# Float64 weight conversion in half pieces, six pieces cast on GpSimd, and x loads queued behind a slice's weights

## The chip, the cores and the metric

The kernel runs on one core of one Trainium2 chip. The metric is the device time of one execution in microseconds (us); with several runs the median is given. A core has TensorE (matrix products; "PE" in the profile, its weight loads "PEld"), VectorE ("DVE"), ScalarE ("ACT"), GpSimd ("POOL") and SyncE ("SP"), whose queue issues nearly all DMA transfers. Each engine works through its own instructions in their order. TensorE's granted clock has two levels, 1.2 and 2.4 GHz; the profile gives its mean in a stretch as a share of the higher one.

## The reference

Three parts in a row: attention with a decay, a gated FFN whose weights are float64, and a mixture of eight experts whose gate is balanced over tokens and experts.

```python
scores = scale * np.matmul(q, k.transpose(0, 1, 3, 2))
scores = np.where(causal, -1000000000.0, scores + decay)
attn = np.exp(scores - max) / sum              # 4 batches, 8 heads, 576 x 64
x = np.matmul(attn, v)                          # to 2304 tokens x 512
g, val = x @ w_gate, x @ w_val                  # 512 -> 1536, weights in float64
x = (silu(g) * val) @ w_out
logits = x @ moe2_w_gate                        # 8 experts
P = softmax, then 8 rounds of dividing by sums over experts and over tokens
out = sum over e of P[:, e] * (max(x @ w1[e], 0) @ w2[e])    # 512 -> 1024 -> 512
```

Every product is made from three fp32r products: each operand is a high word (a cast to fp32r) and a low word, the rest of the subtraction (`rest`).

## The kernel before

Attention of batch 0 runs alone (to about 75 us). Then attention of batch n+1 and the first FFN of batch n run merged, step by step, by a list of costs (`merge`): the first such pair to 247 us, the other two to 540 us, and the FFN of the last batch to 675 us. From there the second FFN runs in three phases over the tokens (to 1188, about 1660 and 2143 us), each phase through all slices of the experts' weights, forwards or backwards. Phase 0 reads the experts' weights (`w1`, `w2`), builds their word and sum forms and saves them to DRAM (`save` into `wq`); phases 1 and 2 read those forms back, slice by slice (`back`: `w1h`, `w1l`, `w2h`, `w2l`, `sh`, `sl`).

**Conversion.** The first FFN's weights lie in DRAM as the bits of float64, in 18 pieces of 128 partitions x 1024 values (4096 16-bit words). [...] The steps of a piece:

- the load `st<-wf` (L114, on SP; tile `st` in three buffers, and `st4` for every fourth piece, so that the load of a piece waits for an earlier piece's last reader);
- VectorE masks the exponent of the top word into `lead` (L129);
- ScalarE scales and rebases it with a Relu (L131);
- VectorE puts the sign back in `lead` (L132, 16-bit, 1024 columns) and shifts the middle word and joins it with `lead` (L134, 32-bit, 1024 columns), after which `v`, a view of `st`, holds fp32 values;
- for each half of 512 columns ScalarE casts to the high word (L139) and GpSimd subtracts for the low word (L167, `rest`), both into a tile of the ring `w` (6 buffers);
- the finished piece is stored to DRAM as `wsplit`, 1 MB, for the other three batches: pieces 0 to 5 in one go after batch 0's attention (L648), the later ones at once (L144).

Pieces 0 to 5 are converted at fixed points of batch 0's attention (`TURNS`; `ROWS` has six entries, so `i < len(ROWS)` means pieces 0 to 5) and kept in `w` as `ready` for the first FFN products; pieces 6 to 17 are converted by `load(s)` inside `moe_unit(0)`, one slice ahead of its use. A scheduler places the instructions of an engine by its own model of times, within the dependences and the orders that `issue_after` sets, so an instruction of piece 8 can stand inside batch 0's attention.

**Attention's names.** `ps_s` scores, `np`/`mn` (L297 on VectorE: decay, mask and row maximum; L302 on ScalarE: exponentials and their sums), `ps_t`/`pt` (transposes of the exponentials and their copies to SBUF, L423, L431, L436), `ps_o` (product with v, L451), `bt` (output, L455, L465), `xh`/`xl` (its high and low word, the FFN's input). In the FFN `pm` are the up products, `th`, `ah`, `al` the activation and its words, `py` the down products (L175 is the line of all three-term products).

**Translation of x.** The second FFN multiplies 2x2 blocks in seven products instead of eight, and its input is kept in DRAM (`xd`) and brought into seven forms by `xlate(2)` for phase 2 (`xload` and `xforms` make those of phases 0 and 1). It has four parts: two loads `xq<-xd` (L750), four subtractions on VectorE (L699), then seven times a cast to `h` on ScalarE (L734), a `rest` on GpSimd and a store `xo<-h` (L738). `h` has two buffers, so the third cast of a part waits for the first store to land. `last_w[0]` is the last weight load of phase 0 that `load2` issued; `issue_after(last_w[0].ins)` keeps an instruction behind it in the queue. In the second FFN `pa` are the up products (L937), which ScalarE moves to SBUF as `u` (L944).

Of the kernel before, what the change touches and what calls it, by code (L numbers as in the profile page):

```python
# [8 lines left out]
F32 = mybir.dt.float32  # L9
# [5 lines left out]
ALU = mybir.AluOpType  # L15
# [18 lines left out]
def attention_two_ffns(ctx: ExitStack, tc: tile.TileContext, qkT, vt, f, wf, g2, w1, w2, out):  # L34
    nc = tc.nc
# [11 lines left out]
    HP = 512  # L47
# [31 lines left out]
    for rows, c in ((slice(0, 64), 0), (slice(64, P), 64)):  # L79
        nc.vector.tensor_copy(out=maskd[rows], in_=maskf[rows, rows])  # L80
        nc.vector.tensor_reduce(
            out=picks[rows], in_=ident[rows, c:c + 3 * NG].rearrange("p (n j) -> p n j", j=3),
# [24 lines left out]
    def wload0(i, behind=None):  # L107
        if i % 4 == 2:
            st = stp.tile([P, 8 * HP + 4], U16, tag="st4", name="st4")
        else:  # L110
            st = cvp.tile([P, 8 * HP + 4], U16, tag="st", name="st", bufs=3)
        behind = behind or last_st[0]
        with tc.issue_after(behind.ins):
            last_st[0] = nc.sync.dma_start(out=st[:, 1:1 + 8 * HP], in_=wf[i].bitcast(U16))  # L114
        return st

    def convert(i):
        base = bases[:, 1:2] if i % 3 == 2 else bases[:, 0:1]
        W = 2 * HP
        st = sts.pop(i, None) or wload0(i)  # L120

        def words(dt):
            return st.bitcast(dt)[:, 0:2 * W].rearrange("p (i t) -> p i t", t=2)[:, :, 1]
        mid, v = words(U32), words(F32)
        top = st[:, 4:4 + 4 * W].rearrange("p (i t) -> p i t", t=4)[:, :, 0]
        lead = leads[i % 2]
        g = lead.bitcast(U16).rearrange("p (i t) -> p i t", t=2)[:, :, 1]
        with tc.issue_after(rows[i].ins) if i < len(ROWS) else ExitStack():
            nc.vector.tensor_scalar(out=g, in0=top, scalar1=0x7fff, scalar2=None, op0=ALU.bitwise_and)  # L129

        nc.scalar.activation(out=g, in_=g, func=AF.Relu, scale=8.0, bias=base)  # L131
        nc.vector.scalar_tensor_tensor(  # L132
            out=g, in0=top, scalar=0x8000, in1=g, op0=ALU.bitwise_and, op1=ALU.bitwise_or)
        nc.vector.scalar_tensor_tensor(  # L134
            out=mid, in0=mid, scalar=13, in1=lead, op0=ALU.logical_shift_right, op1=ALU.bitwise_or)
        t = wring.tile([P, 2, 2, HP], F32R, tag="w", name="w")
        halves = [slice(j * HP, (j + 1) * HP) for j in range(2)]
        for j, h in enumerate(halves):
            nc.scalar.copy(out=t[:, j, 0], in_=v[:, h])  # L139
            rest(t[:, j, 1], v[:, h], t[:, j, 0])  # L140
        if i < len(ROWS):
            stores.append((i, t))
        else:
            nc.sync.dma_start(out=wsplit[i], in_=t.bitcast(F32))  # L144
        return t
# [9 lines left out]
    ROWS = (3, 8, 15, 18, 22, 25)  # L155
# [9 lines left out]
    def rest(out, src, hi, eng=None):  # L165

        return (eng or nc.gpsimd).tensor_tensor(out=out, in0=src, in1=hi.bitcast(F32), op=ALU.subtract)  # L167
# [43 lines left out]
    for j in range(3):  # L211
        src = left if j else ct[0:B * H]
# [4 lines left out]
    for e in range(2):  # L217
        spread_in = nc.sync.dma_start(
            out=spread[64 * e:64 * e + 3 * NG],
            in_=cumt[16 * e:16 * e + NG].rearrange("n j s -> (n j) s"))  # L220
# [402 lines left out]
    with ExitStack() as hold:  # L623
        room = banks(hold, 2, 3)
        idle = room[1].tile([P, 512], F32, tag="t", name="idle")
        for _ in range(WARM):
            nc.tensor.matmul(out=idle[:, 0:P], lhsT=ident, rhs=ident, start=True, stop=True)
        for n, (_, fn) in enumerate(attn_unit(0, *room)):
            fn()
            for i in LOADS.get(n, ()):  # L630
                sts[i] = wload0(i, spread_in if i == 1 else last_qk[0])
            if n in ROWS:
                rows.append(last_step[0])
            if n in TURNS:
                w0.append(convert(len(w0)))
# [10 lines left out]
    with tc.issue_after(last_qk[0].ins):  # L646
        for i, t in stores:
            nc.sync.dma_start(out=wsplit[i], in_=t.bitcast(F32))  # L648
    merge(second, moe_unit(0, convert, w0), lead=LA)
    first.close()  # L650
    cdp = at_ctx.enter_context(pool("cdp", 2, side="right"))
# [43 lines left out]
    def xsums(quarters, ts):  # L695
        b11, b12, b21, b22 = quarters
        t4, t1, t2, t3 = ts
        for o, x, y in ((t1, b12, b11), (t3, b22, b12), (t2, b22, t1), (t4, b21, t2)):
            nc.vector.tensor_tensor(out=o, in0=x, in1=y, op=ALU.subtract)  # L699
        return b11, b21, b22, t4, t1, t2, t3  # L700
# [28 lines left out]
    def xwords(srcs, n, place):  # L729
        hs_ = []  # L730
        for f in range(NF + 1):
            if f < NF:
                hs_.append(sk.tile([P, 2, HG], F32R, tag="h", name="h", bufs=2)[:, :, 0:n])
                nc.scalar.copy(out=hs_[f][:, 0], in_=srcs[f])  # L734
            if f:
                h = hs_[f - 1]
                rest_next(h[:, 1], srcs[f - 1], h[:, 0])
                nc.sync.dma_start(out=place(f - 1), in_=h.bitcast(F32))  # L738
                yield

    def xlate(p):

        n = HG // 2
        for k in range(2):
            for c in range(2):
                st = wst.tile([P, KD, FS], F32, tag="w1", name="xq")[:, :, 0:n].rearrange("p (i j) n -> p i j n", i=2)
                for j in range(2):
                    b, n0 = divmod(p * GT + j * HG + c * n, S)
                    src = xd[b].rearrange("p (i k) n -> p i k n", i=2)[:, :, k, n0:n0 + n]
                    nc.sync.dma_start(out=st[:, :, j], in_=src)  # L750
                yield
                t = wst.tile([P, FS // P, DM], F32, tag="w2", name="xu").rearrange("p f (c n) -> p (f c) n", c=2)
                quarters = [st[:, i, j] for i in range(2) for j in range(2)]
                srcs = xsums(quarters, [t[:, i, 0:n] for i in range(4)])
                yield
                cols = slice(c * n, (c + 1) * n)
                yield from xwords(srcs, n, lambda f: xo[p][:, f, :, k, cols])
# [29 lines left out]
    last_w = [None]  # L787
# [26 lines left out]
    def keep1(i, ts):  # L814
        w1s[slices[i][1:]] = [t.rearrange("p k (f c) -> p f k c", f=NF) for t in ts]
        return w1s[slices[i][1:]]
# [75 lines left out]
    def back(n, i):  # L892
        if i >= len(slices) or i % NS < 2 or i < NS:
            return
        key = slices[i][1:]
        ts = (tiles1, tiles2)[n](i)
        for t, src in zip(ts, wq[(n,) + key]):
            nc.sync.dma_start(out=t.bitcast(F32), in_=src)
        if n:
            w2s[key] = ts  # L900
        else:
            keep1(i, ts)

    def weights(i):
        if i == NS:
            save(1, i - 1)
        back(0, i + 1)
        back(1, i - 1)
# [283 lines left out]
    def ending():  # L1192
        i = len(slices) - 1
        back(1, i)
        for f in zipped(fast(i - 1), form(i)):
            f()
        for t in range(TP):
            slow(i, t)
# [55 lines left out]
    list(make(0, 0))  # L1254
    later = xforms(1)
    last = xlate(2)
    for i in range(len(slices)):
        if i == NS:
# [13 lines left out]
        if 24 <= i < 24 + TP:  # L1272
            t = i - 24
# [42 lines left out]
```

## Time and profile before

| | |
|---|---|
| median of 3 runs | 2146.72 us (2146.15 to 2149.76) |
| the profiled execution | 2145.42 us, of it 2143.6 us span |
| TensorE busy | 2117.2 us, 99%, mean granted clock 0.997 |
| VectorE busy | 1387.9 us, 65% |
| ScalarE busy | 966.5 us, 45% |
| GpSimd busy | 1314.9 us, 61% |
| DMA | 558.09 MB, mean 260 GB/s |

The times come from whole executions; the span is from the first to the last instruction in the trace. Busy shares are means over stages with different limits. In the rows below a time is in us; "DVE lead L129 <- DMA st<-wf" reads: VectorE's instruction of line 129, which writes `lead`, stood idle until a DMA that wrote `st` had landed. Lines are those of the kernel before. In the changed kernel L132 and L134 are L136 and L138, L139 is L140, L167 is L170, and lines behind are 3 or 4 higher.

### The profile page before, as it was taken

The numbers are of one execution on the slowest core, as the hardware profiler recorded it, in microseconds if no ns is written. First come the engines' busy times: TensorE is split into PE (matmuls) and PEld (weight loads), VectorE is DVE, ScalarE is ACT, GpSimd is POOL, SyncE is SP. The second block draws the span as 40 slices with busy tenths as digits, with TensorE's granted clock in tenths as the row PEclk, the third lists the DMA queues.
The fourth block names the chain that finished last, engine by engine and source line by source line (L and its number), as shares of the span: only waits on it lengthen the run. The fifth ranks groups of instructions, "written<-read, shape, count | busy, mean of one in ns | idle before, by whom it ended". The sixth has DMA issues, their size and how long they took to land.

```text
span 2143.6 us, 38167 instructions
## 1 busy us (share of the span) xinstructions
PE 2117.2 (99%) x14191; PEld 1995.5 (93%) x14191; DVE 1387.9 (65%) x3031; ACT 966.5 (45%) x1940; POOL 1314.9 (61%) x1175
## 2 busy tenths in 40 slices
PE   8999999999999999999999999999999999999999
PEld 5778999999999898888888899999999999999998
DVE  7765444534444887877877476666666666666666
ACT  8655444443323464454444443444444434444442
POOL 3445535432633768777775686766766767667664
PEclk9999999999999999999999999999999999999999
DMA  7766655754752989999888787776767667667664
GB/s 226 287 226 208 219 177 176 228 165 145 269 192 98 347 323 340 351 335 349 327 333 326 272 319 271 273 266 256 287 253 299 227 257 278 259 261 288 255 265 182
DMA packets 165259, 558.09 MB, mean 260 GB/s; under 512 B 17892, under 2 KB 62224, under 8 KB 153552
## 3 DMA queue, kind: packets, MB, share of 16 engines
q1 hardware_dynamic: 165072, 555.64, 70.9%
q8 instruction: 112, 1.84, 0.3%
q14 instruction: 75, 0.61, 0.1%
HBM read 390.04 MB, written 165.54 MB: 259 GB/s over the span
## 4 chain that ended last, share of the span: by engine, by line
PE 88%; DMA 4%; ACT 3%; POOL 2%; issue 1%; DVE 1%; SPq 0%; POOLq 0%; ACTq 0%; DVEq 0%
PE pa L937 32%; PE py L1064 21%; PE py L175 18%; PE pm L175 12%; DMA st<-wf 2%; PE ps_o L451 2%; PE ps_t L423 1%; PE ps_s L327 1%; DMA xo<-h 1%; ACT np L302 1%; ACT lead L131 1%; DMA xf<-xo 0%; DMA xst<-xd 0%; ACT w L139 0%; POOL w L167 0%
## 5 line engine op out<-in xcount | busy, mean ns | idle before, releaser
L1038 DVE SCALAR_TENSOR_TENSOR acc<-py,zmaskd,acc 128x256 f32<-128x256 f32 (+1 forms) x1128 | 545.7, 526 | 255.6 <-PE py L1064 241.5
L937 PE MATMUL pa<-xf,w1h 128*128 128x384 f32 x2688 | 687.3, 336 | 3.8 <-ACT u L944 3.5
L937 PEld LDWEIGHTS pa<-xf,w1h 128*128 128x128 f32 x2688 | 469.6, 189 | 23.6 <-ACT u L944 5.2
L937 PE MATMUL pa<-xf,w1l 128*128 128x384 f32 x1344 | 449.9, 335 | 0.0
L175 PE MATMUL pm<-xh,w 128*128 128x288 f32 x1536 | 326.4, 298 | 1.3 <-ACT xh L466 1.0
L944 ACT COPY u<-pa 128x384 f32<-128x384 f32 x192 | 91.9, 479 | 431.4 <-PE pa L937 431.4
L1018 POOL TENSOR_TENSOR td<-rr 128x768 f32<-128x768 f32 x62 | 114.8, 1852 | 257.9 <-ACT rr L957 257.9
L175 PEld LDWEIGHTS pm<-xh,w 128*128 128x128 f32 x1536 | 251.9, 189 | 7.4 <-issue 2.8
L937 PEld LDWEIGHTS pa<-xf,w1l 128*128 128x128 f32 x1344 | 252.3, 188 | 0.0
L175 PE MATMUL pm<-xl,w 128*128 128x288 f32 x768 | 227.7, 297 | 0.0
L167 POOL TENSOR_TENSOR al<-th,ah 128x288 fp32r<-128x288 f32 x96 | 80.8, 843 | 227.1 <-ACT ah L552 227.1
L167 POOL TENSOR_TENSOR al<-td,ah 128x1536 fp32r<-128x1536 f32 x62 | 217.9, 3515 | 3.4 <-ACT ah L1031 2.4
L1064 PE MATMUL py<-sh,al 128*128 128x256 f32 x744 | 209.6, 282 | 0.0
L1064 PE MATMUL py<-sl,ah 128*128 128x256 f32 x744 | 209.2, 281 | 0.0
L1064 PE MATMUL py<-sh,ah 128*128 128x256 f32 x744 | 208.6, 280 | 0.0
L167 POOL TENSOR_TENSOR al<-rr,ah 128x384 fp32r<-128x384 f32 (+1 forms) x130 | 186.2, 1433 | 8.1 <-ACT ah L1009 5.9
L175 PE MATMUL py<-ah,w 128*128 128x288 f32 x768 | 176.3, 302 | 3.7 <-DVE th L550 3.2
L175 PE MATMUL py<-w2h,al 128*128 128x512 f32 x408 | 161.9, 397 | 0.0
L175 PE MATMUL py<-w2l,ah 128*128 128x512 f32 x408 | 161.1, 395 | 0.0
L175 PE MATMUL py<-w2h,ah 128*128 128x512 f32 x408 | 159.2, 390 | 0.0
L1064 PE MATMUL py<-w2h,ah 128*128 128x256 f32 x558 | 157.1, 282 | 0.5 <-DVE acc L1038 0.5
L1064 PE MATMUL py<-w2h,al 128*128 128x256 f32 x558 | 157.4, 282 | 0.0
(191 smaller groups left out, 4593.3 us busy)
## 6 DMA issues: line engine op xcount, KB each, us to landing
w<-wsplit SPq DMA_DIRECT2D x54, 1024.0 KB, 6.7
w1h<-wq SPq DMA_DIRECT2D x60, 896.0 KB, 7.6
w1l<-wq SPq DMA_DIRECT2D x60, 896.0 KB, 9.4
w<-w SPq DMA_DIRECT2D x64, 512.0 KB, 5.3
sh<-wq SPq DMA_DIRECT2D x60, 512.0 KB, 4.4
sl<-wq SPq DMA_DIRECT2D x60, 512.0 KB, 3.5
w2l<-wq SPq DMA_DIRECT2D x60, 512.0 KB, 4.6
w2h<-wq SPq DMA_DIRECT2D x60, 512.0 KB, 5.8
```

The costliest lines, as they stand in the source:

```text
L131: nc.scalar.activation(out=g, in_=g, func=AF.Relu, scale=8.0, bias=base)
L167: return (eng or nc.gpsimd).tensor_tensor(out=out, in0=src, in1=hi.bitcast(F32), op=ALU.subtract)
L175: ins = nc.tensor.matmul(out=ps, lhsT=a, rhs=b, start=(i == 0), stop=(i == n - 1))
L302: last_exp[0] = nc.scalar.activation(out=pt, in_=pt, func=AF.Exp, scale=-1.0, bias=bias, accum_out=sms[hp % 2][:, col:col + 1])
L327: one = nc.tensor.matmul(out=ps[:, e, 0:w], lhsT=a[:, q0:L], rhs=k[:, 0:w], start=(k is kh), stop=(k is kl))
L423: nc.tensor.transpose(ps[:, j * P:(j + 1) * P], pt[:, c:c + P], ident)
L451: one = nc.tensor.matmul(out=po[rows, c0:w], lhsT=vs[:, j, rows], rhs=pts[rng][:, j, e, c0:w], start=(j == 0), stop=(j == n - 1))
L937: last_pa[0] = nc.tensor.matmul(out=ps, lhsT=w[:, MW[m - 1], k], rhs=x[m - 1][:, hl, k], start=(first and n == 0), stop=(n == len(ops) - 1 ...
L944: nc.scalar.copy(out=t, in_=ps)
L1018: nc.gpsimd.tensor_tensor(out=t[:, 0:2], in0=r[:, 1:3], in1=r[:, 0:2], op=sub)
L1038: nc.vector.scalar_tensor_tensor(out=a, in0=src, scalar=lg[:, t, e:e + 1], in1=a, op0=ALU.mult, op1=ALU.add)
L1064: last_pa[0] = nc.tensor.matmul(out=ps, lhsT=x, rhs=y, start=(first and k == 0), stop=(k == 2), skip_group_check=not first)
```

## The change

Three edits.

- In `convert`, VectorE's last two steps are issued in halves of 512 columns: sign and join of the first half, its cast and its rests, then the second half. The rests go by 256 columns, four a piece instead of two of 512.
- The casts of pieces 0 to 5 are issued to GpSimd instead of ScalarE.
- In `xlate`, the loads of x stand behind `last_w[0]`, and `back` now sets it at every weight load of phases 1 and 2, too.

```diff
-        nc.vector.scalar_tensor_tensor(
-            out=g, in0=top, scalar=0x8000, in1=g, op0=ALU.bitwise_and, op1=ALU.bitwise_or)
-        nc.vector.scalar_tensor_tensor(
-            out=mid, in0=mid, scalar=13, in1=lead, op0=ALU.logical_shift_right, op1=ALU.bitwise_or)
         t = wring.tile([P, 2, 2, HP], F32R, tag="w", name="w")
         halves = [slice(j * HP, (j + 1) * HP) for j in range(2)]
+        cast = nc.gpsimd.tensor_copy if i < len(ROWS) else nc.scalar.copy
         for j, h in enumerate(halves):
-            nc.scalar.copy(out=t[:, j, 0], in_=v[:, h])
-            rest(t[:, j, 1], v[:, h], t[:, j, 0])
+            nc.vector.scalar_tensor_tensor(
+                out=g[:, h], in0=top[:, h], scalar=0x8000, in1=g[:, h], op0=ALU.bitwise_and, op1=ALU.bitwise_or)
+            nc.vector.scalar_tensor_tensor(
+                out=mid[:, h], in0=mid[:, h], scalar=13, in1=lead[:, h], op0=ALU.logical_shift_right, op1=ALU.bitwise_or)
+            cast(out=t[:, j, 0], in_=v[:, h])
+            for q in range(2):
+                c = slice(q * HP // 2, (q + 1) * HP // 2)
+                rest(t[:, j, 1, c], v[:, h][:, c], t[:, j, 0, c])
...
-                    nc.sync.dma_start(out=st[:, :, j], in_=src)
+                    with tc.issue_after(last_w[0].ins):
+                        nc.sync.dma_start(out=st[:, :, j], in_=src)
...
-            nc.sync.dma_start(out=t.bitcast(F32), in_=src)
+            last_w[0] = nc.sync.dma_start(out=t.bitcast(F32), in_=src)
```

The scheduler moves other instructions along. Three places follow. First VectorE at the end of batch 0's attention, before; `lead_197<-st` at the top is the first step of piece 8, `lead_199<-st` that of piece 7, and `bt` is the attention output that the first FFN products need:

```order
L129 TENSOR_SCALAR lead_197<-st 128x1024
L431 COPY pt_202<-ps_t 128x3x128
L129 TENSOR_SCALAR lead_199<-st 128x1024
L431 COPY pt_202<-ps_t 128x3x128
L132 SCALAR_TENSOR_TENSOR lead_197<-st,lead_197 128x1024
L436 COPY pt_202<-ps_t 128x8x64
L132 SCALAR_TENSOR_TENSOR lead_199<-st,lead_199 128x1024
L134 SCALAR_TENSOR_TENSOR st<-st,lead_197 128x1024
L134 SCALAR_TENSOR_TENSOR st<-st,lead_199 128x1024
L465 TENSOR_TENSOR bt<-ps_r,bt 128x288 x2
```

And VectorE there now:

```order
L434 COPY pt_202<-ps_t 128x3x128
L129 TENSOR_SCALAR lead_199<-st 128x1024
L434 COPY pt_202<-ps_t 128x3x128
L136 SCALAR_TENSOR_TENSOR lead_199<-st,lead_199 128x512 x2
L439 COPY pt_202<-ps_t 128x8x64
L138 SCALAR_TENSOR_TENSOR st<-st,lead_199 128x512 x2
L468 TENSOR_TENSOR bt<-ps_r,bt 128x288 x2
```

Piece 8's three steps have left this place; they now stand among the first FFN products' activations, and its load on SP stands behind five of the six stores of L648 instead of ahead of all six.

Second, VectorE ahead of 125 us, before; the steps of `lead_199` here are those of piece 11, and `np` are row maxima of batch 1's scores:

```order
L129 TENSOR_SCALAR lead_199<-st 128x1024
L551 TENSOR_TENSOR th<-pm,th 128x288
L431 COPY pt_202<-ps_t 128x3x128
L132 SCALAR_TENSOR_TENSOR lead_199<-st,lead_199 128x1024
L134 SCALAR_TENSOR_TENSOR st<-st,lead_199 128x1024
L297 ISA np,mn<-ps_s,zmask 128x384
```

And there now:

```order
L129 TENSOR_SCALAR lead_199<-st 128x1024
L434 COPY pt_202<-ps_t 128x3x128
L136 SCALAR_TENSOR_TENSOR lead_199<-st,lead_199 128x512 x2
L138 SCALAR_TENSOR_TENSOR st<-st,lead_199 128x512
L300 ISA np,mn<-ps_s,zmask 128x384
L300 ISA mn 128x1
L300 ISA np,mn<-ps_s,zmask 128x384
L300 ISA mn 128x1
L138 SCALAR_TENSOR_TENSOR st<-st,lead_199 128x512
```

The second half of the last step has moved behind both 384-wide row maxima. Further on, the first step of piece 12 stands directly ahead of the 512-wide row maxima in both orders.

Third, SP's queue where the first pair of x loads stands, before; `wq_31_1` is the saved form of slice 31, the last of phase 0, and L890 saves:

```order
L890 DMA wq_30_0_13478<-w2h 128x1024
L890 DMA wq_30_2_13482<-sh 128x1024
L890 DMA wq_31_0_13474<-w1h 128x1792
L750 DMA xq<-xd_108 128x2x192
L750 DMA xq<-xd_109 128x2x192
L803 DMA w_13442<-w 128x2x512
L890 DMA wq_30_1_13480<-w2l 128x1024
```

And the first pair now, where L902 reads saved forms back in phase 1:

```order
L902 DMA w1h<-wq_25_0_12542 128x1792
L902 DMA w1l<-wq_25_1_12544 128x1792
L902 DMA sl<-wq_26_3_12888 128x1024
L902 DMA sh<-wq_26_2_12886 128x1024
L754 DMA xq<-xd_108 128x2x192
L754 DMA xq<-xd_109 128x2x192
L902 DMA w2l<-wq_26_1_12884 128x1024
L902 DMA w2h<-wq_26_0_12882 128x1024
```

The x loads have moved from the end of phase 0 into phase 1, behind `sl` and `sh` of slice 26 and ahead of its other forms; the second pair stands in the same way at slice 22, and the others follow in the same manner.

## Rows read from the trace of the kernel before

**Rows 1.** The page's first part: busy us (share of the span) xinstructions.

```profile
PE 2117.2 (99%) x14191; PEld 1995.5 (93%) x14191; DVE 1387.9 (65%) x3031; ACT 966.5 (45%) x1940; POOL 1314.9 (61%) x1175
```

**Rows 2.** Busy us by stretches: PE, PEld, DVE, ACT, POOL; then PEclk, DMA share, GB/s.

```profile
126.00:132.80 6.80, 5.67 (x25) 4.19 (x26) 6.41 (x14) 3.81 (x8) 2.47 (x1) 0.50 1.01 428
...
1200.00:1300.00 100.00, 98.37 (x657) 95.96 (x658) 68.56 (x134) 47.25 (x90) 81.83 (x67) 1.00 0.80 287
1300.00:1400.00 100.00, 100.00 (x711) 100.00 (x710) 68.10 (x143) 40.60 (x67) 67.20 (x40) 1.00 0.69 264
```

**Rows 3.** The chain of waits, 0 to 80 us: start, length, what.

```profile
37.44 1.22 ACT w L139 x2
...
39.39 2.26 PE ps_o L451 x20
...
42.61 6.54 DMA st<-wf
49.18 1.69 DVE lead L129
...
52.36 1.33 DVE lead L132
53.71 1.24 DVE st L134
54.97 1.22 ACT w L139 x2
...
56.92 3.54 PE ps_o L451 x20
...
65.99 1.13 ACT w L139 x2
...
68.35 1.43 ACT lead L131
...
73.87 0.70 DVE st L134
...
75.45 0.66 PE pm L175 x3
```

**Rows 4.** Instructions on tile st: duration ns min/median/max, first and last start us.

```profile
L139 ACT CAST w<-st x36: 650/662/703, 20.5 to 204.7; 128x512 fp32r<-128x512 f32 x36
L167 POOL TENSOR_TENSOR w<-st,w x36: 1291/1316/2330, 21.3 to 206.2; 128x512 fp32r<-128x512 f32 x36
...
L129 DVE TENSOR_SCALAR lead<-st x18: 748/848/1675, 14.1 to 168.8; 128x1024 uint16<-128x1024 uint16 x18
```

**Rows 5.** Timeline of TensorE: start us, us, instruction [idle before <-releaser].

```profile
70.52 0.33 PE L423 MATMUL ps_t<-ident,np 128*128 128x128 f32 x1 [1.15 <-ACT pt L431]
71.01 2.27 PE L451 MATMUL ps_o<-pt,vs 128*64 128x320 f32 x20 [0.16 <-ACT pt L431]
...
75.45 0.66 PE L175 MATMUL pm<-xh,w 128*128 128x288 f32 x3 [0.97 <-ACT xh L466]
...
127.13 2.19 PE L370 MATMUL ps_s<-qk 64*64 64x288 f32 x8 [3.08 <-DVE mn L297]
```

**Rows 6.** Timeline of VectorE, the same columns.

```profile
46.77 0.42 DVE L297 CUSTOM_DVE_ANT_0 np<-ps_s,zmask 128x256 f32<-128x256 f32 x1
...
54.85 0.68 DVE L297 CUSTOM_DVE_ANT_0 np<-ps_s,zmask 128x512 f32<-128x512 f32 x1
...
125.14 0.75 DVE L129 TENSOR_SCALAR lead<-st 128x1024 uint16<-128x1024 uint16 x1 [5.10 <-DMA st<-wf]
```

**Rows 7.** GpSimd by line and shape: busy us, mean ns of one.

```profile
L167 POOL TENSOR_TENSOR sl<-sd,sh 128x256 fp32r<-128x256 f32 x128 | 98.9, 808 | 2.6 <-ACT sh L874 2.6
...
L1281 POOL MEMSET acc<- 128x512 f32 x6 | 3.0, 526 | 0.0
```

**Rows 8.** Loads of x: instructions of line 750, as in rows 4.

```profile
L750 SPq DMA_DIRECT2D xq<-xd x8: 529/530/649, 1150.1 to 1237.7; - x8
```

**Rows 9.** Waits, 1180 to 1235 us: us in total, times, longest us.

```profile
ACT h L734 <- DMA xo<-h: 8.8, 10, 3.0
...
ACT u L944 <- PE pa L937: 7.1, 5, 3.0
...
PE pa L937 <- ACT u L944: 3.0, 4, 1.4
```

## The prediction

> **What bounds the kernel now.** The page's first part says TensorE: busy 99% of the span [rows 1]. A share of the whole span cannot price an edit, so the second view is the same by stretches: from 1300 us on, in the second FFN, TensorE is busy for the whole 100 us, and between 1200 and 1300 it loses 1.63 us [rows 2]. What this change can win is therefore only the time in which TensorE waits or runs at its low clock, and the change touches three places of that kind: the first 76 us (attention of batch 0, with the conversion of weight pieces 0 to 8 inside it), the conversion of the other pieces (6 to 17), and the border of phase 0 and phase 1 of the second FFN, 1180 to 1235 us.
>
> In the first 76 us the view to read is the chain of waits [rows 3]. It does not run along TensorE: it alternates between a weight piece's load (6.54 us), the four conversion steps on VectorE and ScalarE, ScalarE's cast pair "w" (1.22 us), the softmax pieces "np" behind it, and only then the products ps_o. Twice, at 37.44 and at 54.97, the cast pair stands directly ahead of the np on which ps_o hangs. At the end the chain goes over the second conversion step of two pieces to bt, xh and the first FFN product at 75.45. TensorE's own timeline shows the waits: 1.15 and 0.16 us at 70.5 to 71.0, 0.97 us at 75.45, and 3.08 us at 127.13 [rows 5]. The wait at 127.13 is for VectorE's row maximum, and VectorE stood 5.10 us in front of it at the first step of piece 12, whose load had not landed [rows 6]. There TensorE's granted clock falls to 0.50 (the 1.2 GHz level) for 126.0 to 132.8 us [rows 2]; half of those 6.8 us is the most that the low clock can have cost.
>
> For the sum I use the profiled execution: 2145.42 us, of which 2143.6 is the span. The median of the runs is 2146.72, so 1.30 us is added at the end.
>
> **The change, part by part.**
>
> *Casts of pieces 0 to 5 go to GpSimd.* ScalarE loses six pairs of 1.22 us, 7.3 us of its time [rows 3, 4]. GpSimd gets twelve casts of 128x512. It has no such cast in the trace. The nearest rows are its memory set of the same width, 0.526 us, and its two-input subtraction of the same width, 1.291 us at least [rows 4, 7]; a copy reads one input, between the two, so I take 1.0 us, and 0.5 to 1.3 as ends: 12 us in all (6.3 to 15.6). GpSimd's own queue then holds cast and subtraction of a piece back to back, and the low word xl of the attention's output stands between them; it is covered as long as the first FFN products don't ask for it.
>
> *Two steps of VectorE in halves, subtractions in quarters of a piece.* A softmax piece of 256 columns takes 0.42 us on VectorE and one of 512 takes 0.68 [rows 6]: one cut costs 2 x 0.42 - 0.68 = 0.16 us at most, and nothing at least, if the fixed part overlaps. I take 0.12, near the row. Two cuts a piece are 0.24 us of VectorE. On GpSimd two of 256 columns take 2 x 0.808 = 1.62 against 1.29 to 1.32 for 512 [rows 4, 7], 0.3 us a cut, 0.6 us a piece. In exchange the cast of the first half may start when half of the second step is done, about 0.6 us earlier (half of the 1.24 us at 53.71).
>
> *What these two do in the first 76 us.* Station one, 37.44 us: without the pair in front, np and ps_o start up to 1.22 us earlier, but np's own input stands on VectorE behind step two, now 0.24 us longer, and is ready soon after. I take -0.7; SP's load of piece 4 (42.61) hangs on that ps_o and moves with it. Station two, 54.97 us: the same pair, again not the full 1.22, since np there waits for VectorE behind steps 52.36 and 53.71; -0.6 net of the 0.24. Station three, 63 to 75 us: the pair at 65.99 (1.13 us) is gone. The order moves one thing more: piece 8's load stands behind five of the 1 MB stores of converted pieces instead of ahead of them, and its whole conversion (0.85 + 1.33 + 1.24 us of VectorE and 1.43 us of ScalarE, [rows 3, 4]) leaves the tail of attention 0 and stands behind the first FFN products. That takes what lies ahead of bt (0.70 us at 73.87) off VectorE. The waits of TensorE there sum to 2.3 us [rows 5]; the transposes still have to wait for their copies, and part of the gain is that of stations one and two arriving again as a wait; I take -0.7. Sum -2.0 us. Ends: -5, if nearly every pair counts (7.3 - 6 x 0.24 = 5.9, less 0.9 for a pair that is not on the chain), and +1, if GpSimd's 12 us turn into waits for xl or for a free load buffer.
>
> *The same two steps for pieces 6 to 17.* Twelve times 0.24 us on VectorE and 0.6 us on GpSimd lie beside TensorE's products: cost 0, at most +1 if one of them stands ahead of a row maximum. Ahead of the wait at 127.13 the order helps: of piece 11 the last half step now stands behind the 384-wide row maxima instead of ahead of them (half of 1.24 us). The first step of piece 12 keeps its place directly ahead of the 512-wide ones, so the 5.10 us wait for its load stays, earlier by what piece 11 gives back. I take -0.6; ends -6.5 (wait of 3.08 us and half of the 6.8 us at low clock both gone) and +3 (the load lands later).
>
> *The x loads behind the slice's weights.* Before, the eight loads of all four parts of the translation of x for phase 2 start between 1150.1 and 1237.7 us [rows 8], with phase 0's last weight stores and the results' stores in the same queue. ScalarE waits there 8.8 us in ten pieces for an earlier store of h to land, and TensorE waits 3.0 us for ScalarE's u [rows 9]. In the new order the first pair stands on SP behind sl and sh of the fourth slice that is read back, and the other parts follow every four to five slices. So that wait is relieved; as ScalarE itself waits 7.1 us for TensorE in the same stretch, not every one of the 3.0 us is the casts' doing. I take -1.6 of 3.0. Each part still has seven casts in ScalarE's queue, the third and later waiting for a store to land, with u behind them. The fourth part's casts lie behind the last load, after 1237.7, and TensorE lost only 1.63 us in the whole hundred from 1200 on [rows 2], so each part costs little: +0.15, four times, +0.6. Sum -1.0; ends -3.0 and +2.
>
> *All together:* -2.0 - 0.6 - 1.0 = -3.6; 2145.42 - 3.6 = 2141.8, and 1.3 for the median: 2143.1 us.
>
> **A rule against it.** VectorE's first step takes 0.748 us at best and 1.675 at worst, and GpSimd's subtraction 1.291 and 2.330 [rows 4]; the 1.69 us one at 49.18 lies on the chain [rows 3]. The Trainium skill, page "Advanced Engine Details and Errata", section "VectorE Performance Modes", says that the second port of VectorE is shared with GpSimd and that instructions of both using it block each other; the spread of those rows agrees with it. If it held for every moved cast, rival 2 below would be the result.
>
> **The rivals.**
>
> 1. *The chain follows the casts (faster).* For it: the pair stands on the chain three times, and ScalarE has no other long work there. Against it: behind each pair something is ready only shortly before. If the first 76 us give -5 instead of -2, the time is 2140.1; if instead the wait at 127 and its low clock vanish (-6.5 for -0.6), it is 2137.2. Chance 0.25, some 2136 to 2141.
>
> 2. *GpSimd slows VectorE in attention 0.* Twelve more microseconds of GpSimd lie beside VectorE's steps. If the first step of five pieces goes from 0.75 to 1.68 us, that is +4.6 on the chain: 2147.7, no change to be seen. For it: the 1.69 us on the chain; against it: GpSimd already ran beside VectorE there, and this was one piece. Chance 0.14.
>
> 3. *The x casts stall the steady phase (slower).* In phase 1 TensorE has no idle time that could swallow a wait. If in each of the four parts one wait of ScalarE for a store of h, 3.0 us at the longest [rows 9], passes through u to TensorE, that is +12 instead of +0.6: 2154.5. It decides the sign from 2.1 us a part on. Against it: the fourth part's stretch in before, and DMA is busy 0.69 there instead of 0.80 [rows 2]. Chance 0.11.
>
> **How the numbers follow.** The forecast has 0.50, with 2140 to 2147 as its own range. About 0.2% (4.3 us) is what a measurement of this kernel can tell from no change: 2142.4 and 2151.0 are the borders. A third of the forecast lies under 2142.4 (0.17), with rival 1 that makes faster 0.42; slower is rival 3, 0.11; the rest, 0.47, is within. The range from 2137.0 to 2148.5 leaves out rival 3 and the far end of rival 1.
>
> **What would show it.** Right: twelve casts of about 1 us on GpSimd before 80 us; the first FFN product at about 73.5 instead of 75.45; a wait of 2 to 3 us of TensorE left near 125, with the low clock behind it; no wait for u over 0.5 us between 1186 and 1230, and TensorE at 100 of 100 us in every later stretch. Wrong: a new wait for xl before 80, first steps over 1.5 us on VectorE in a row, TensorE under 99 where the x casts stand in phase 1, or casts of under 0.6 us with the first FFN product before 71.

## The result: slower by 0.9%, and the profile after

| | before | after |
|---|---|---|
| median | 2146.15 us (5 runs) | 2165.22 us (5 runs, 2162.28 to 2168.1) |
| ratio | 1 | 1.0086, 95% interval 1.0074 to 1.0098 |
| profiled span | 2143.6 us | 2163.4 us |

The forecast was 2143.1 us with a range of 2137.0 to 2148.5. The span grew by 19.8 us. Where, the busy time by stretches tells first. These rows are the changed kernel's and answer [rows 2]; the columns are the same (PE, PEld, DVE, ACT, POOL, then PEclk, DMA share, GB/s):

```profile
126.00:132.80 6.80, 5.83 (x46) 4.69 (x47) 6.76 (x16) 4.17 (x10) 1.45 (x1) 1.00 1.02 429
1200.00:1300.00 100.00, 96.08 (x625) 93.38 (x624) 62.29 (x118) 39.94 (x70) 66.46 (x46) 0.98 0.63 233
1300.00:1400.00 100.00, 99.45 (x706) 99.13 (x705) 70.36 (x145) 44.09 (x75) 74.57 (x49) 1.00 0.78 295
1400.00:1500.00 100.00, 93.11 (x633) 91.99 (x632) 71.66 (x134) 39.60 (x73) 65.24 (x49) 0.97 0.71 262
```

And the last of them in the kernel before, which had not been shown:

```profile
1400.00:1500.00 100.00, 100.00 (x712) 100.00 (x712) 67.90 (x144) 41.96 (x67) 67.28 (x40) 1.00 0.68 263
```

The steady stretches are no longer full. From 1200 to 1500 us TensorE issues 625 + 706 + 633 = 1964 products instead of 657 + 711 + 712 = 2080 [rows 2]: 116 fewer, at 711 in 100 us some 16 us of work. The first product `pa` of the second FFN starts 5.6 us later (681.8 us instead of 676.2), so of the 19.8 us 14.2 are lost behind it. So most of the loss lies in phase 1, where the x loads went. What TensorE waits for there (waits of the changed kernel, 1240 to 1500 us: us in total, times, longest us):

```profile
PE py L1068 <- DVE acc L1042: 10.8, 7, 2.9
```

It waits for VectorE's accumulations, not for ScalarE's u. VectorE's timeline at the first of these places, and GpSimd's beside it (start us, us, instruction, idle before it):

```profile
1271.08 1.59 DVE L702 TENSOR_TENSOR xu<-xq 128x192 f32<-128x192 f32 x2 [1.46 <-DMA xq<-xd]
1272.60 0.47 DVE L1042 SCALAR_TENSOR_TENSOR acc<-py,zmaskd,acc 128x256 f32<-128x256 f32 x1
1272.99 1.60 DVE L702 TENSOR_TENSOR xu<-xq,xu 128x192 f32<-128x192 f32 x1
1274.51 0.47 DVE L1042 SCALAR_TENSOR_TENSOR acc<-py,zmaskd,acc 128x256 f32<-128x256 f32 x1
1274.91 3.21 DVE L702 TENSOR_TENSOR xu<-xq,xu 128x192 f32<-128x192 f32 x1
```

```profile
1272.42 1.96 POOL L170 TENSOR_TENSOR al<-rr,ah 128x768 fp32r<-128x768 f32 x1
1274.34 3.57 POOL L170 TENSOR_TENSOR al<-td,ah 128x1536 fp32r<-128x1536 f32 x1
```

Two things are to be seen. VectorE stood 1.46 us at the first subtraction of x, until the x load landed. And the last two subtractions, of 192 columns each, take 1.60 and 3.21 us, each until 0.21 us after the GpSimd instruction beside it ends (1272.42 + 1.96 = 1274.38 against 1272.99 + 1.60 = 1274.59; 1274.34 + 3.57 = 1277.91 against 1274.91 + 3.21 = 1278.12). The same holds for all four parts: of their 16 subtractions 15 start beside a running GpSimd instruction and end 0.21 to 0.22 us after it, and the one that meets none takes 343 ns. The accumulations between them, which read one operand from PSUM, take their 0.47 us as ever. Over all parts the last two subtractions of a part, those that read `xu`, took (ns min/median/max):

```profile
L702 DVE TENSOR_TENSOR xu<-xq,xu x8: 343/1610/3214, 1273.0 to 1479.0; 128x192 f32<-128x192 f32 x8
```

The other loss, the 5.9 us by which the first FFN is late at 310 us, shows in two waits of TensorE's, at 175.57 and at 274. In TensorE's timeline the first of these was 0.45 us in the kernel before and is 4.08 us in the changed one; in the waits of 260 to 285 us the second was 3.2 and is 4.2 us:

```profile
174.82 0.40 PE L175 MATMUL py<-ah,w 128*128 128x288 f32 x1 [0.45 <-DVE xa L568]
175.57 0.40 PE L178 MATMUL py<-ah,w 128*128 128x288 f32 x1 [4.08 <-DVE xa L571]
```

```profile
PE py L175 <- DVE th L550: 3.2, 1, 3.2
PE py L178 <- DVE th L553: 4.2, 1, 4.2
```

A stretch at the low clock follows the wait at 175.57 and that of the first part in phase 1 (1276.37 to 1279.43):

```profile
176.00:180.00 4.00, 4.00 (x22) 3.53 (x21) 1.85 (x8) 2.93 (x9) 2.96 (x5) 0.57 0.02 4
1279.00:1283.00 4.00, 3.57 (x16) 3.58 (x17) 3.21 (x8) 0.51 (x2) 0.00 (x0) 0.57 0.03 8
```

In the first 76 us nearly nothing is won: the first FFN product starts at 75.04 instead of 75.45. (It is the first of those that need the end of batch 0's attention; 27 others ran from 62.07 us on in the kernel before.) A difference of 0.4 us between two traces says little there. In three runs further down the code up to that product is that of the kernel before, and it starts at 74.19, 78.11 and 74.31 us (the x edit alone, the same with GpSimd's instructions in pieces, the x loads a slice ahead):

```profile
74.19 0.66 PE L175 MATMUL pm<-xh,w 128*128 128x288 f32 x3 [0.82 <-ACT xh L466]
78.11 0.66 PE L175 MATMUL pm<-xh,w 128*128 128x288 f32 x3 [0.38 <-ACT xh L466]
74.31 0.67 PE L175 MATMUL pm<-xh,w 128*128 128x288 f32 x3 [1.04 <-ACT xh L466]
```

### The profile page after: what moved, and what is told of

Its sections match the earlier page's. It is cut to its first block, busy times and chain, and to the rows that moved or that the text cites. A ratio compares the mean times of both kernels' runs of the same rounds, so it can differ in the third digit from the quotient of the medians.

```text
span 2163.4 us, 38233 instructions
## 1 busy us (share of the span) xinstructions
PE 2122.4 (98%) x14191; PEld 1999.7 (92%) x14191; DVE 1407.3 (65%) x3067; ACT 960.9 (44%) x1928; POOL 1329.9 (61%) x1223
## 4 chain that ended last, share of the span: by engine, by line
PE 87%; DVE 4%; DMA 4%; POOL 2%; ACT 2%; issue 1%; SPq 0%; DVEq 0%; ACTq 0%; POOLq 0%
PE pa L941 32%; PE py L1068 20%; PE py L178 19%; PE pm L178 11%; DMA st<-wf 2%; PE ps_o L454 2%; PE ps_t L426 1%; DMA xq<-xd 1%; PE ps_s L330 1%; DVE xu L702 1%; DVE st L138 1%; DVE lead L136 1%; ACT lead L131 1%; DVE acc L1042 1%; POOL w L170 1%
## 5 line engine op out<-in xcount | busy, mean ns | idle before, releaser
L1068 PE MATMUL py<-sh,ah 128*128 128x256 f32 x744 | 210.5, 283 | 10.8 <-DVE acc L1042 10.8
```

The lines of the kernel that those rows point to most:

```text
L1068: last_pa[0] = nc.tensor.matmul(out=ps, lhsT=x, rhs=y, start=(first and k == 0), stop=(k == 2), skip_group_check=not first)
```

## Experiments

Ratios are to the kernel before on the same chip, with their 95% interval.

**Each edit alone.** First the x edit alone:

```diff
+                    with tc.issue_after(last_w[0].ins):
                         nc.sync.dma_start(out=st[:, :, j], in_=src)
...
-            nc.sync.dma_start(out=t.bitcast(F32), in_=src)
+            last_w[0] = nc.sync.dma_start(out=t.bitcast(F32), in_=src)
```

> The kernel before with the third edit alone: the x loads behind the slice's weights. Theory X (VectorE's subtractions of x, which now stand among the accumulations of phase 1, make TensorE wait): four waits of 3 to 4 us in phase 1 as in the changed kernel, three of them followed by a stretch at the 1.2 GHz level (1.7 us each), less 2.6 us at the border of the phases: about +14, 2160 us. Rival C (most of the loss comes from the conversion edits): within 3 us of before, 2143 to 2149 us.

1.0071 (1.0053 to 1.0088), 2159.15 us, and 10.3 us of waits for the accumulations between 1240 and 1500:

```profile
PE py L1065 <- DVE acc L1039: 10.3, 7, 2.7
```

Theory X stands: this edit is most of the loss.

Then both conversion edits without it (the full diff of `convert`):

> The changed kernel without the third edit: the x loads as before, both conversion edits kept. Theory X: the loss that is left is that of the first 310 us, +5.7, so 2152 us, and no wait in phase 1 after 1240 us. Rival C: 2158 us or more.

1.0040 (1.0025 to 1.0055), 2153.11 us, with the 4.1 us wait near 175 us. Within its interval that is the 5.7 us expected.

Of these the halves and the 256-wide rests together, casts left on ScalarE:

```diff
+        cast = nc.scalar.copy
```

> The kernel before with VectorE's last two conversion steps in halves and the rests by 256 columns; all casts stay on ScalarE. Theory H (more and reordered VectorE instructions make the conversion of pieces 6 to 17 late, the 4 us wait at 175 us in the changed kernel): +4 to +6, 2150 to 2152 us. Rival G (the casts on GpSimd are the loss): within 2 us of before.

1.0040 (1.0025 to 1.0055), with the same wait of 4.1 us. And the casts alone:

```diff
+        cast = nc.gpsimd.tensor_copy if i < len(ROWS) else nc.scalar.copy
         for j, h in enumerate(halves):
-            nc.scalar.copy(out=t[:, j, 0], in_=v[:, h])
+            cast(out=t[:, j, 0], in_=v[:, h])
```

> The kernel before with the casts of pieces 0 to 5 on GpSimd, nothing in halves. Theory H: the first FFN product at 75.45 moves by less than 1 us either way, and the total is within 2 us of before, since VectorE's steps and the loads stand on the chain in place of the casts. Rival G: +4 to +6 us, from GpSimd's casts beside VectorE's steps.

0.9976 (0.9966 to 0.9985), 2139.80 us. Neither theory: the first FFN product did move by less than 1 us (75.52), but the total gained 5 us, more than the 2 us of theory H. Where that comes from is taken up below. The loss of the conversion edits is the halves', on VectorE or on GpSimd.

**Which halves.** VectorE's two steps in halves with 512-wide rests, and the other way round, the 256-wide rests with nothing else:

```diff
-            rest(t[:, j, 1], v[:, h], t[:, j, 0])
+            for q in range(2):
+                c = slice(q * HP // 2, (q + 1) * HP // 2)
+                rest(t[:, j, 1, c], v[:, h][:, c], t[:, j, 0, c])
```

> The kernel before with VectorE's last two conversion steps in halves alone; rests stay 512 wide, casts on ScalarE. Theory H1 (the halves on VectorE, by the order they bring, make the wait at 175 us): the 4.2 us wait there and the low clock behind it are in this run, 2150 to 2153 us. Rival H2 (the rests by 256 columns on GpSimd): 2144 to 2147 us, and no such wait.

> The kernel before with the rests of the conversion by 256 columns alone. H1: 2144 to 2147 us, within 0.1% of before. H2: 2150 to 2153 us with a wait of about 4 us near 175 us.

1.0030 (1.0017 to 1.0043) for the halves on VectorE, but with other waits than expected: 1.6 us near 179 us instead of 4.2, and a first FFN product at 79.45 us. And 1.0017 (1.0007 to 1.0026) for the rests alone, with a wait of 2.8 us at 176 us. Both theories fall: either edit alone slows the kernel, and the smallest of all, twice as many GpSimd instructions off TensorE's path, brings a wait at the same place. What the kernels with that wait share is found in TensorE's order: all four with the 256-wide rests (the changed kernel, both conversion edits, halves with rests, rests alone) have one order of batch 1's scores among the first FFN's products, and the kernel before another. In theirs the scheduler puts the scores later:

| batch 1's scores stand behind product | kernel | longest wait of TensorE at 165 to 185 us | ratio |
|---|---|---|---|
| 390, 408, 444, 468 | before | 0.4 us | 1 |
| 396, 420, 456, 480 | both conversion edits | 4.1 us | 1.0040 |
| 396, 420, 456, 480 | rests alone | 2.8 us | 1.0017 |
| 396, 420, 462, 480 | halves on VectorE alone | 1.6 us | 1.0030 |

The halves alone have a third order. Their loss stays open: the wait of 1.6 us is smaller than the loss, and the product at 79.45 us lies only 1.3 us beyond the 74.19 to 78.11 us of the kernels with the old conversion.

In the kernel before TensorE has attention products (173.0 us) just ahead of the products that wait for VectorE's xa; in the other order it runs through FFN products only and arrives at 171.5 us, while VectorE still stands in the conversion of a piece whose load has just landed (168.5 us in the changed kernel, 168.8 in the kernel before).

**The order alone.** One number of the merge, the lead of batch 1's attention, moves the scores without touching an instruction of the conversion:

```diff
-    LA, LB, LC = 1.0, 1.2, 1.2
+    LA, LB, LC = 0.95, 1.2, 1.2
```

With 0.95 the rests alone, and both conversion edits, get the scores back behind 390, 408, 444, 468 (the ones ahead of these stay behind 318 and 336 instead of 300, 324 and 348, and of the later ones those from product 588 on stand elsewhere, too):

> The rests by 256 columns alone, as in the run that had them alone (2150 us), and one number of the merge changed (the lead of batch 1's attention from 1.0 to 0.95), by which the scores of batch 1 stand behind 390, 408, 444 and 468 of the first FFN's products again, as in the kernel before, instead of 396, 420, 456 and 480. Theory O (the loss of the conversion edits is the order in which the scheduler puts scores among FFN products): the wait of 3 to 4 us at 175 us and the low clock behind it are gone, 2144 to 2147 us. Rival S (the loss is the added instructions themselves): still 2149 us or more.

> Both conversion edits without the x edit, as in the run that had them (2153 us), with the same lead of 0.95 and the same order of scores. Theory O: no wait over 2 us at 175 us, 2145 to 2149 us. Rival S: 2152 us or more.

1.0000 (0.9990 to 1.0010) and 1.0009 (0.9998 to 1.0019). With the rests a wait of 1.5 us is left in that stretch. With both edits in and the four scores in their old places, TensorE's waits between 150 and 185 us are (waits, as above):

```profile
PE py L178 <- DVE th L554: 0.4, 1, 0.4
PE pm L178 <- DVE th L553: 0.4, 1, 0.4
```

and its timeline shows the scores that stand there again, right ahead of the down products:

```profile
170.32 0.49 PE L335 MATMUL ps_s<-qk 64*128 64x128 f32 x4
170.65 0.22 PE L316 MATMUL ps_s<-spread,pick 64*128 64x128 bf16 x2
171.26 0.40 PE L178 MATMUL py<-ah,w 128*128 128x288 f32 x1 [0.39 <-DVE th L554]
```

And the reverse, the kernel before with a lead of 0.90 and no other edit:

> The kernel before with the lead of batch 1's attention at 0.90 and nothing else, by which its scores move among the FFN products (behind 318, 336, 372, 402, 432, 462, 480 instead of 300, 324, 348, 390, 408, 444, 468). Theory O: the time moves by 2 to 8 us, with no instruction added, 2148 to 2154 us if the wait at 175 us comes, as in the other orders with scores at 480. Rival S: within 2 us of before.

1.0028 (1.0017 to 1.0040), 2151.68 us, with this in the waits of 165 to 185 us:

```profile
PE py L175 <- DVE th L550: 3.1, 1, 3.1
```

So theory O holds in both directions: the order alone costs 0.28% with no instruction changed, and in the order of lead 0.95 the conversion edits cost nothing that goes beyond the interval. Two things are not shown. The kernel before was not run with a lead of 0.95, so what that order is worth without the edits is open. And in the one order 396, 420, 456, 480 the ratio is 1.0017 with the rests alone and 1.0040 with the halves as well (their intervals just overlap), so the order may not be all of it there.

**Load or GpSimd, in phase 1.** The x edit alone, with GpSimd's long instructions of phases 1 and 2 in pieces of 384 columns; the x loads stay where they are:

```diff
...
-            rest(l[:, 1:3], r[:, 2:4], h[:, 1:3])
+            for n in (1, 2):
+                rest(l[:, n], r[:, n + 1], h[:, n])
...
-            rest(l[:, 3:7], t, h[:, 3:7])
+            for n in range(4):
+                rest(l[:, 3 + n], t[:, n], h[:, 3 + n])
```

> The x loads behind the weights alone, as the run with that edit alone (2159 us), and GpSimd's long two-input instructions of phases 1 and 2 cut into pieces of 384 columns (the 1536-wide rest into four, the 768-wide rest and difference into two). Theory P (VectorE's subtraction of x cannot run beside GpSimd's and ends only with it): the 3.2 and 1.6 us subtractions of x fall to about 1 us, the waits of TensorE in phase 1 from about 3.8 us a part to under 1, the low clock behind them is gone, 2146 us or less. Rival L (the load of x lands too late, and that is the wait): the load's position is the same, so the waits stay, 2157 us or more.

0.9989 (0.9978 to 1.0000) instead of 1.0071. VectorE still waits for the x loads (5.4 us in four waits), but its subtractions are short and TensorE's waits are a tenth; first the subtractions, then TensorE's waits of 1240 to 1500 us:

```profile
L699 DVE TENSOR_TENSOR xu<-xq,xu x8: 753/777/781, 1267.4 to 1462.9; 128x192 f32<-128x192 f32 x8
```

```profile
PE py L1068 <- DVE acc L1042: 1.1, 3, 0.5
```

The late load is therefore not the cause; the length of the GpSimd instruction beside the subtraction is. The second test moves the subtractions instead:

```diff
+            with tc.issue_after(last_acc[0].ins):
+                srcs = xsums(quarters, [t[:, i, 0:n] for i in range(4)])
...
+                if f == 4 and m + 1 < len(places):
+                    nxt = xq(*places[m + 1])
```

> As the run with the x loads alone, but a part's loads are issued a slice ahead of its subtractions, which are kept behind an accumulation of their own slice. Theory L: VectorE no longer waits for the load and TensorE's waits in phase 1 vanish, 2146 us or less. Theory P: no wait for the load, but subtractions of 1.6 and 3.2 us wherever GpSimd works beside them, and still 2 to 4 us of waits a part, 2153 to 2160 us.

0.9986 (0.9973 to 0.9999), 2142.31 us. Both theories had said something else in part: VectorE doesn't wait for the load any more, as L expects, but the subtractions are short, too, 0.70 to 1.00 us for those that read `xu`, because in their new place GpSimd works on 384- and 768-wide pieces (1.03 to 1.99 us) and not on the 1536-wide one. The subtractions and TensorE's waits of 1240 to 1500 us:

```profile
L699 DVE TENSOR_TENSOR xu<-xq,xu x8: 704/844/998, 1291.5 to 1471.2; 128x192 f32<-128x192 f32 x8
```

```profile
PE pa L951 <- ACT u L958: 0.5, 1, 0.5
```

This run alone would not have told the two apart.

**The casts' 5 us.** The casts alone had come with an order of scores of their own (402, 444, 468, 492). Two other leads, 0.90 and 1.1, give the same edit two other orders:

> The casts of pieces 0 to 5 on GpSimd alone, with the lead of batch 1's attention at 0.90, by which its scores stand behind 312, 330, 390, 408, 444, 468 of the first FFN's products instead of 318, 336, 402, 444, 468, 492 in the run with the casts alone. Theory O2 (the 5.2 us gained there came with the order of scores, not with ScalarE's relief): 2143 to 2148 us here. Rival K (the casts themselves gain it): 2137 to 2142 us.

> The same with the lead at 1.1: scores behind 444, 468, 504 and later ones moved. Theory O2: any time between 2140 and 2150 us, and not the same as with the lead at 0.90. Rival K: 2137 to 2142 us again.

1.0000 (0.9990 to 1.0009) at 0.90, and 0.9980 (0.9971 to 0.9990) at 1.1. The gain goes and comes with the order, as theory O2 has it. What goes and comes is the wait at 269 us, 3.2 us in the kernel before and with a low-clock stretch behind it. TensorE from 255 to 295 us in the kernel before, with the casts alone, and with the casts at leads 0.90 and 1.1:

```profile
255.00:295.00 40.00, 36.78 (x269) 34.20 (x268) 10.55 (x38) 18.59 (x50) 16.16 (x15) 0.96 0.48 158
255.00:295.00 40.00, 39.77 (x306) 37.40 (x305) 16.19 (x59) 20.00 (x59) 19.22 (x19) 1.00 0.78 229
255.00:295.00 40.00, 36.30 (x266) 33.22 (x265) 11.48 (x43) 18.43 (x49) 14.11 (x14) 0.96 0.44 146
255.00:295.00 40.00, 40.00 (x306) 37.25 (x305) 14.67 (x53) 20.77 (x60) 17.52 (x16) 1.00 0.74 221
```

From product 390 on, three kernels with three different edits stand in one order, that of 390, 408, 444, 468 and 588: the rests and both conversion edits at lead 0.95, and the casts at 0.90. Their ratios are 1.0000, 1.0009 and 1.0000. That the casts by themselves gain nothing is still argued and not shown: without them lead 0.90 came to 1.0028, in another order, so at either lead the kernel with the casts was the faster one, by 0.24 and 0.28%.

**The whole, and the best.** The changed kernel with all three edits, x loads a slice ahead and lead 0.95:

> The changed kernel with all three edits, mended at the two places found: x loads a slice ahead of their subtractions, and the lead at 0.95, which puts the scores where the kernel before has them. If the two places are the whole loss: 2165 less 14 to 17 in phase 1 less 4 to 6 at 175 and 270 us, 2143 to 2146 us. If something is still unexplained: 2148 us or more.

0.9990 (0.9979 to 1.0001), 2144.43 us: the two places were the whole loss. The x loads a slice ahead alone came to 0.9986, so what the conversion edits still cost lies within the intervals. And the casts with the x loads a slice ahead, without halves, at the old lead:

> The casts on GpSimd alone (5.2 us faster than before) together with the x loads a slice ahead of their subtractions (3 us faster). If the two gains add, being 1000 us apart: 2136 to 2138 us, 0.9960 of before. If the gain of the second run was that of a different first 300 us only: 2139 to 2141 us.

0.9962 (0.9949 to 0.9975), 2137.06 us, the fastest kernel here: the two gains add.

## Why the prediction was wrong

*The x loads, forecast -1.0 us, measured about +14.* Half of this term was right: the waits for u at the border fell from 3.0 us [rows 9] to 1.2, where -1.6 was forecast:

```profile
PE pa L941 <- ACT u L948: 1.2, 2, 0.6
```

The step that failed is "each part costs little: +0.15". It counted seven casts on ScalarE and left out the part's four subtractions on VectorE, which are moved with the loads. They stand among the accumulations that TensorE waits for, and beside GpSimd's longest instructions. Four parts cost 10.8 us of waits, and three of them a stretch at 1.2 GHz: the clock is 0.57 from 1279 to 1283 us, 0.72 from 1418 to 1424, 0.66 from 1483 to 1488, and 1.00 behind the second part (1336 to 1344). Rival 3 had the place and the sign, and its 2154.5 us was not far off for this edit alone (2159), but its mechanism was another: ScalarE does wait for stores of h, 6.6 us in six waits between 1240 and 1500, but TensorE waits for u not once there. The argument from the fourth part, which in the kernel before had run after 1237.7 without a loss, failed for the same reason: there the subtractions had stood beside shorter instructions of GpSimd (1.85 us at the longest instead of 3.57) and taken 0.70 and 0.78 us for the two that read xu.

*The rule against it.* The prediction named it and applied it to the conversion alone. [rows 4] showed the spread there; its rows hold none of the subtractions of x. Here the trace is plain: a subtraction with both operands in SBUF ends with the GpSimd instruction beside it, and an accumulation with one operand in PSUM is not touched. The Trainium skill, page "SBUF — State Buffer", section "Who interferes with whom", says that a VectorE instruction with two SBUF inputs contends with a GpSimd instruction that reads SBUF, and calls the lock on the ports that both share an exclusive one; that the engine which issues first keeps them for its whole instruction it says of VectorE's two-port modes. The trace agrees, and shows such a block for these subtractions, too: 3.21 us beside 3.57 us, and once the pieces were cut 0.78 us at most for the subtractions that read xu and 1.17 us for the other two.

*Pieces 6 to 17, forecast 0 and -0.6 at 127 us, measured +5.9 by 310 us.* The instructions' own cost was about 0, as forecast (1.0009 with both edits and the four scores in their old places). The step that failed is that these instructions "lie beside TensorE's products: cost 0": it took TensorE's order as given. The scheduler answers more or longer instructions with another order of scores, and kernels with other orders came out 4 to 5 us faster or 4 to 9 us slower (ratios 0.9976, 0.9980, 1.0017, 1.0028, 1.0030, 1.0040 twice); the 1.0028 has the order alone, the others an edit as well. The wait at 127 us stayed (3.03 us, forecast 2 to 3), but this time no low clock followed it: 126.0 to 132.8 us ran at 1.00 in the first rows above, against 0.50 in [rows 2]. That is not the edits' doing: with both conversion edits alone the wait is 3.1 us, and 129.6 to 133.0 us behind it ran at 0.50.

*The first 76 us, forecast -2.0, measured -0.4* (one pair of traces, at a place that moves by 3.9 us in runs of the same code). ScalarE lost its six pairs, and the chain of waits went over to VectorE. These rows answer [rows 3]:

```profile
36.71 1.18 DVE st L138 x2
37.89 0.60 DVE np L300
...
39.11 0.61 DVE pt L439
...
39.86 2.28 PE ps_o L454 x20
...
43.09 6.11 DMA st<-wf
...
70.35 0.68 DVE pt L439
...
71.17 2.29 PE ps_o L454 x20
```

Behind step two VectorE does np and a copy of the transposes, and ps_o starts at 39.86 instead of 39.39, at 71.17 instead of 71.01. Stations one and two were priced at -0.7 and -0.6 because np's own input "is ready soon after". It is ready hardly sooner than the cast pair was done: ScalarE now stands 0.83 us for the row maximum and starts its exponentials at 38.53 instead of 38.56, and ps_o then waits for the copy of VectorE's behind it. In the kernel before that copy (L436) stood in the same place behind np, at 56.07, and was not counted. ScalarE at station one before and now, and VectorE's copy before:

```profile
38.56 0.73 ACT L302 ACTIVATE np<-np,mn 128x512 f32<-128x512 f32 x1
38.53 0.72 ACT L305 ACTIVATE np<-np,mn 128x512 f32<-128x512 f32 x1 [0.83 <-DVE mn L300]
```

```profile
56.07 0.69 DVE L436 COPY pt<-ps_t 128x512 f32<-128x512 f32 x1
```

With the casts alone the product starts at 75.52, no earlier either. GpSimd's cast itself was bounded rightly at 0.5 to 1.3 us, and the 1.0 us taken was high:

```profile
L140 POOL CAST w<-st x12: 641/854/1114, 20.1 to 67.3; 128x512 fp32r<-128x512 f32 x12
```

Rivals 1 and 2 did not come: no station gained its pair, and no first step took 1.68 us (1.38 us at most on the chain before 70 us). With the casts alone rival 2's sign was there, one first step of 1.88 us on the chain at 32.50, and the kernel was the faster one all the same.

## What to carry to other kernels

Of a step that is moved, list every instruction on every engine, and ask of each what will run beside it there: the VectorE subtraction with two SBUF operands lasted here until the GpSimd instruction that it met had ended, so such a one belongs beside short ones, or the long ones are cut. Where a scheduler places work, a small edit's own price can be near nothing while the order it sets off is worth several microseconds: compare TensorE's order first, and give the same edit, and the kernel without it, two or three other orders before the edit is credited or blamed. A bound that is taken off one engine is worth only the distance to the next engine in the chain, which the row behind the removed one shows.

## What the runs showed of the hardware

In the kernel with the casts alone the 128x512 GpSimd cast took 632 to 667 ns, against 1282 ns at least for the two-input subtraction of the same width. The 128x192 subtraction of VectorE took from 343 to 3214 ns by its neighbour on GpSimd. The neighbour's kind counts: in the kernel before, three of these subtractions (1201 to 1202 us) lie beside a GpSimd memory set, which reads nothing, and take 343 to 357 ns. And waits of like length do not always bring the low clock: 3.03 us at 127 us were followed by full clock in the changed kernel, 3.08 us at the same place by 6.8 us at 0.50 in the kernel before.
